# A causal convolution and a low-rank mixer on one core: batch 1 takes the 64-by-32 convolution, with its shifted x copied by DMA

## The chip, the cores and the metric

The kernel runs on one core of a Trainium2 chip. The metric is device time in microseconds (us) of one execution. The kernel before takes 325.4 us (median of three runs, 325.24 to 325.87). The engines of the core are named as in the profile: PE (TensorE, matrix products), PEld (its weight loads), DVE (VectorE), ACT (ScalarE), POOL (GpSimd) and SP (SyncE, which here only issues DMAs).

## The reference

The input x has 8 batches of 4224 rows of 192 channels. Each of 8 heads (24 channels) is convolved along the rows with 7 causal taps, the softmax of the head's weights. The result goes through a low-rank mixing along the rows (U, then V), which is added back, and through a two-layer network per row, which is added too.

```python
def _attn_ref(x, weight):                     # x: 8 x 4224 x 192, weight: 8 heads x 7 taps
    w = weight - np.max(weight, axis=-1, keepdims=True)
    w = np.exp(w)
    w = w / (np.sum(w, axis=-1, keepdims=True) + 1e-09)
    pad = K - 1
    x_pad = np.concatenate([np.zeros((B, pad, D), dtype=np.float32), x], axis=1)
    idx = np.arange(S)[:, None] + np.arange(K)[None, :]
    x_unf = x_pad[:, idx, :].reshape(B, S, K, H, group)
    out = np.einsum('hk,bskhg->bshg', w, x_unf)
    return out.reshape(B, S, D).astype(np.float32)

def _moe_ref(x, U, V, w_ch1, w_ch2):          # U: 4224 x 32, V: 32 x 4224, w_ch1: 192 x 768, w_ch2: 768 x 192
    xt = x.transpose(0, 2, 1)
    h = xt @ U @ V
    u = x + h.transpose(0, 2, 1)
    ch = np.maximum(u @ w_ch1, 0.0) @ w_ch2
    return (u + ch).astype(np.float32)

# reference: _moe_ref(x=_attn_ref(x, weight), U, V, w_ch1, w_ch2)
```

## The kernel before

A batch is 33 tiles of 128 rows, and the 8 batches make 264 tiles, handled in 33 groups of 8. For each batch the steps are: load x (in bfloat16), convolve it into y ("c", or "d" for batch 1), multiply by U ("t"), sum the partial results ("s"). For each group: multiply by V and add to y, giving u, and transpose u by DMA ("h"); then the two layers, `w1` and `w2`. Batches do not end where groups end: group 4 holds the last tile of batch 0 and seven tiles of batch 1, group 8 two tiles of batch 1 and six of batch 2. Batch 0 has a code of its own, ahead of all this, which the change leaves alone.

x of one batch lies in SBUF in blocks of 64 rows: partitions 0 to 63 hold the first 32 blocks, partitions 64 to 127 the other 34. `XP` are the four parts in which a batch is loaded. There are two buffers for x (`xs`, bufs=2), one for the shifted copy of x (`xbs`, bufs=1), three for y, seven for u, five for the transposed u, and eight PSUM banks.

```python
    NB0 = 32
    NB1 = S // HB - NB0

    def x_tile(b):
        xt[b] = xs.tile([P, NB1 + 1, D], BF16, name="x_sb")

    def x_zero(b, eng):
        eng.memzero(xt[b][0:HB, 0, :])

    def x_part(b, r, s0, s1):

        blk = NB0 * r + s0 - 1
        return nc.gpsimd.dma_start(
            out=xt[b][HB * r : HB * r + HB, s0:s1, :],
            in_=x[b, blk * HB : (blk + s1 - s0) * HB, :].rearrange("(j p) d -> p j d", p=HB),
        )

    XP = [(0, 1, 17), (0, 17, NB0 + 1), (1, 0, 18), (1, 18, NB1 + 1)]
```

There are two forms of the convolution. `conv` takes tiles of 64 rows by 64 columns of PE and needs, for every block, the block itself and the one before it, with two matrices of weights. `conv32` takes tiles of 64 by 32 and computes 32 output rows at a time from a window of 64 rows that holds all that they need. For every second group of 32 output rows this window is a block of x as loaded; for the others it is moved by 32 rows, and for these `x_shift` makes a second copy of x on GpSimd, in six steps: partitions 0 to 31 and 64 to 95 from the next block ("same"), partitions 32 to 63 and 96 to 127 from the same block ("ahead", written over what "same" put there). Both forms issue 64 matmuls and 16 evictions for a batch; the string `engs` says which engine (A: ACT, D: DVE) evicts.

```python
    xbt = [None] * B

    def x_shift(b):


        xbt[b] = xbs.tile([P, NB1, D], BF16, name="xb_sb")

        def same(s0, s1, *rest):
            def step():
                nc.gpsimd.tensor_copy(out=xbt[b][:, s0:s1, :], in_=xt[b][:, s0 + 1 : s1 + 1, :])
                for t0, t1 in rest:
                    nc.gpsimd.tensor_copy(
                        out=xbt[b][HB : HB + QB, t0:t1, :],
                        in_=xt[b][HB : HB + QB, t0 + 1 : t1 + 1, :],
                    )

            return step

        def ahead(r, s0, s1):
            def step():
                q = slice(HB * r + QB, HB * r + HB)
                nc.gpsimd.tensor_copy(out=xbt[b][q, s0:s1, :], in_=xt[b][q, s0:s1, :])

            return step

        m = NB0 // 2
        return [
            same(0, m),
            same(m, NB0, (NB0, NB1)),
            ahead(0, 0, m),
            ahead(0, m, NB0),
            ahead(1, 0, m),
            ahead(1, m, NB1),
        ]

    steps = []

    def conv32(b, h0, nh, engs):


        if yt[b] is None:
            yt[b] = ys.tile([P, NT, D], BF16, name="y_sb")
        nk = (NB0 // 2, NB1 // 2)
        for n in range(nh):
            h = h0 + n
            hs = slice(h * GS, h * GS + GS)
            pp = [bank(), bank()]
            for cg in range(4):
                t, w, st = (
                    (xt[b], bands[h // HQ][:, h % HQ, QB : 2 * QB], 1 + cg // 2)
                    if cg % 2
                    else (xbt[b], band2[:, h, :], cg // 2)
                )
                for r in range(2):
                    hr = slice(HB * r, HB * r + HB)
                    nc.tensor.matmul(
                        out=pp[r][QB * cg : QB * cg + QB, 0 : nk[r] * GS],
                        lhsT=w[hr],
                        rhs=t[hr, st : st + 2 * nk[r] - 1 : 2, hs],
                        start=True,
                        stop=True,
                        tile_position=(HB * r, QB * cg),
                    )
            # ... (two evictions, to yt[b] for the two halves, on engs[(2 * n + part) % len(engs)])

    def conv(b, h0, nh, rs, engs, ks=((0, NB0 // 2), (0, NB1 // 2)), pp=None):

        nk = {r: ks[r][1] - ks[r][0] for r in rs}
        if pp is None:
            pp = {r: bank() for r in rs}
        w = nh * GS
        for hh in range(nh):
            h = h0 + hh
            for halo in range(2):
                for r in rs:
                    for c in range(2):
                        st = 1 - halo + c + 2 * ks[r][0]
                        last = nc.tensor.matmul(
                            out=pp[r][HB * c : HB * c + HB, 0 : nk[r] * w].rearrange(
                                "p (k a) -> p k a", a=w
                            )[:, :, hh * GS : hh * GS + GS],
                            lhsT=bands[h // HQ][
                                HB * r : HB * r + HB, h % HQ, HB * halo : HB * halo + HB
                            ],
                            rhs=xt[b][HB * r : HB * r + HB, st : st + 2 * nk[r] - 1 : 2, h * GS : h * GS + GS],
                            start=(halo == 0),
                            stop=(halo == 1),
                            tile_position=(HB * r, HB * c),
                        )
        # ... (one eviction for each r, as in conv32)
        return last
```

The parts of a group, and the two layers:

```python
    # h_group(g): 8 matmuls (tiles of 32 by 128) into 4 or more banks, then DVE's additions to y, which give u

    def transp(g):
        uTt[g] = uts.tile([P, 4, 3, P], BF16, name="uT")
        return nc.sync.dma_start_transpose(
            out=uTt[g][:].rearrange("p i c t -> p (i c) t"),
            in_=ut[g][:].rearrange("p i c f k -> p (i c f k)"),
        )

    # ... (yT_part and hT_part: groups 0 and 1, transposed on PE)

    RELU = ["AD", "AD", "AA", "AD", "AD", "AD"]
    RELU0 = ["AA", "AD", "AA", "AD", "AA", "AD"]

    def w1(g, pat):
        rl = rls.tile([P, MC, 2, 4 * P], BF16, name="rl_sb")
        rlt[g] = rl
        ends = []
        # ... (order: for each m of MC = 6 the three c; pps: its banks)
        for m, c in order:
            if c == 0:
                pps[m] = [bank(), bank()]
            for hf in range(2):
                last = nc.tensor.matmul(
                    out=pps[m][hf][:],
                    lhsT=W1_sb[HB * hf : HB * hf + HB, c, m * P : (m + 1) * P],
                    rhs=uTt[g][HB * hf : HB * hf + HB, :, c, :],
                    start=(c == 0),
                    stop=(c == 2),
                    tile_position=(HB * hf, 0),
                )
            if c < 2:
                continue
            pp = pps[m]
            ends.append(last)
            # ... (relu of the two banks into rl, on ACT or DVE as pat[m] says)
        return ends

    # ...

    def w2(g, t0, n):

        hf, i = t0 // 4, t0 % 4
        cps = bank()
        for a in range(n):
            for m in range(MC):
                last = nc.tensor.matmul(
                    out=cps[:, a * D : (a + 1) * D],
                    lhsT=rlt[g][:, m, hf, (i + a) * P : (i + a + 1) * P],
                    rhs=W2_sb[:, m, :],
                    start=(m == 0),
                    stop=(m == MC - 1),
                )
        done_w2.append(last)
        # ... (DVE adds cps to u and gives o)
        # ... (the 192 KB of o are written out from SyncE's queue)
```

The order of the work is a list of slots. A slot has the groups whose `w1` runs, the groups whose `w2` runs after these, and what is put ahead of the quarter p of the `w2`s (a quarter is `w2` on two tiles, 12 matmuls). `LOADS` says after which matmuls of which `w1` the parts of a batch are loaded.

```python
    def x_load(b, q, after):
        if q == 0:
            x_tile(b)
            x_zero(b, nc.gpsimd)
        held(x_part(b, *XP[q]), after)

    SLOTS = [
        ([0], [], {}),
        ([1], [0], {0: ["h0"], 1: ["h3", "l2:2"], 2: ["l2:3"]}),
        ([2], [1], {0: ["d1", "h1"], 1: ["t1"], 3: ["s1"], 4: ["h4", "x2:6"]}),
        ([3], [2], {1: ["h5"], 3: ["h6"]}),
        (
            [4, 5],
            [3, 4, 5],
            {
                0: ["h7"],
                2: ["c2:0:3:AAD"],
                3: ["c2:3:3:AAD"],
                4: ["c2:6:2:A", "x3:4"],
                6: ["t2"],
                8: ["s2"],
                9: ["h8"],
                11: ["h9"],
            },
        ),
    ]
    nh = 10
    for k in range(5, 14):
        gs = list(range(3 * k - 9, 3 * k - 6))
        hs = [f"h{g}" for g in range(nh, min(nh + 3, NG))] + [None] * 3
        nh = min(nh + 3, NG)
        if k == 5:
            at = {
                2: ["c3:0:3:AAD"],
                3: ["c3:3:3:AAD"],
                4: ["c3:6:2:A", "x4:3"],
                5: [hs[0]],
                6: ["t3"],
                8: ["s3", hs[1]],
                11: [hs[2]],
            }
        elif k < 10:
            b = k - 2
            at = {
                1: [f"c{b}:0:3:AAD"],
                2: [f"c{b}:3:3:AAD"],
                3: [f"c{b}:6:2:A"] + ([f"x{b + 1}:3"] if b + 1 < B else []),
                5: [f"t{b}", hs[0]],
                7: [f"s{b}"],
                8: [hs[1]],
                11: [hs[2]],
            }
        else:
            at = {0: [hs[0]], 4: [hs[1]], 8: [hs[2]]}
        SLOTS.append((gs, gs, {p: [w for w in what if w] for p, what in at.items()}))
    assert nh == NG

    LOADS = {2: [(1, 5), (1, 5)], 3: [(4, 1), (4, 4), (5, 1), (5, 4)]}
    for b in range(4, B):
        g = 3 * b - 6
        LOADS[b] = [(g, 0), (g, 3), (g + 1, 0), (g + 1, 3)]

    # ... (batch 0; the first part of batch 1 is loaded here, the other three at its end)

    def do(what):
        if what[0] == "c":
            b, h0, n, engs = what[1:].split(":")
            conv32(int(b), int(h0), int(n), engs)
            return
        if what[0] == "d":
            for h in range(H):
                last = conv(int(what[1:]), h, 1, [0, 1], "AA" if h == 2 else "AD")
            held(transp(3), last)
            return
        if what[0] == "l":
            b, q = (int(v) for v in what[1:].split(":"))
            x_load(b, q, done_w2[-1])
            return
        if what[0] == "x":
            b, n = (int(v) for v in what[1:].split(":"))
            steps.extend(x_shift(b))
            for _ in range(n):
                steps.pop(0)()
            return
        n = int(what[1:])
        if what[0] == "h":
            h_group(n)
            if n > 1 and n != 3:
                transp(n)
        elif what[0] == "t":
            tt_split(n, tt_mm(n, range(NT)))
        else:
            tt_sum(n)

    for gs1, gs2, at in SLOTS:
        for g in gs1:
            ends = w1(g, RELU0 if g == 1 else RELU)
            for b, blocks in LOADS.items():
                for q, (gb, m) in enumerate(blocks):
                    if gb == g:
                        x_load(b, q, ends[m])
                        if steps:
                            steps.pop(0)()
            if g == 0:
                do("h2")
        while steps and gs1 != [3]:
            steps.pop(0)()
        npc = 4 * len(gs2)
        for p in range(npc + 1):
            for what in at.get(p, []):
                do(what)
            if p < npc:
                g, k = gs2[p // 4], p % 4
                if g == NG - 1 and k == 3:
                    w2(g, 6, 1)
                    w2(g, 7, 1)
                else:
                    w2(g, 2 * k, 2)
```

## Time and profile before

| Quantity | Value |
|---|---|
| Time, median of three | 325.4 us |
| Span of the profiled execution | 323.5 us |
| PE busy | 317.1 us (98%) |
| DVE busy | 269.1 us (83%) |
| ACT busy | 170.4 us (53%) |
| POOL busy | 142.7 us (44%) |
| Granted PE clock | 1.00 over the whole span |
| DMA | 53.52 MB, mean 165 GB/s |

The span is the time between the first and the last instruction in the trace; the time of a run is a little longer than it. "Busy" adds up the time in which an engine has an instruction under way; matmuls overlap, so a busy PE is not PE at its peak. In the lists of groups and in the timeline a row gives the line of the kernel (L554 is `w1`'s matmul, L583 `w2`'s, L369 `conv`'s, L339 `conv32`'s, L457 `h_tiles`', L402 the product with U), the engine, the operation, out<-in with their shapes, and how often it ran. A timeline row starts with the start and the length in us and ends, in brackets, with the idle time of the engine ahead of it and what ended it. L256 and L258 are the evictions to y on ACT and DVE; L568 and L570 those of `w1`; L293, L295 and L305 are the copies of `x_shift`; L79 is the issue of a load of x.

### The profile page before, as it was taken

The numbers are of one execution on the slowest core, as the hardware profiler recorded it, in microseconds if no ns is written. First come the engines' busy times: TensorE is split into PE (matmuls) and PEld (weight loads), VectorE is DVE, ScalarE is ACT, GpSimd is POOL, SyncE is SP. The second block draws the span as 40 slices with busy tenths as digits, with TensorE's granted clock in tenths as the row PEclk, the third lists the DMA queues.
The fourth block names the chain that finished last, engine by engine and source line by source line (L and its number), as shares of the span: only waits on it lengthen the run. The fifth ranks groups of instructions, "written<-read, shape, count | busy, mean of one in ns | idle before, by whom it ended". The sixth has DMA issues, their size and how long they took to land.

```text
span 323.5 us, 9584 instructions
## 1 busy us (share of the span) xinstructions
PE 317.1 (98%) x3996; PEld 223.2 (69%) x3996; DVE 269.1 (83%) x551; ACT 170.4 (53%) x344; POOL 142.7 (44%) x111
## 2 busy tenths in 40 slices
PE   6999999999999999999999999999999999999996
PEld 3757676478677647866864784587797497487495
DVE  6769989987977986998798699879898897896864
ACT  1766624860874397088339708824903902912920
POOL 8664179729947694786859497000000000000000
PEclk9999999999999999999999999999999999999999
DMA  8999993999996899699699976139269059048035
GB/s 104 192 192 178 209 211 99 203 195 248 210 153 180 229 175 169 170 162 195 166 238 183 192 162 181 33 112 244 58 168 267 8 149 268 25 121 271 2 119 176
DMA packets 122907, 53.52 MB, mean 165 GB/s; under 512 B 87760, under 2 KB 122832, under 8 KB 122864
## 3 DMA queue, kind: packets, MB, share of 16 engines
q1 hardware_dynamic: 84528, 38.08, 47.0%
q0 software_dynamic: 38192, 14.73, 39.6%
q8 instruction: 31, 0.51, 0.7%
q14 instruction: 12, 0.10, 0.1%
q10 hardware_dynamic: 144, 0.10, 0.1%
HBM read 29.49 MB, written 25.95 MB: 171 GB/s over the span
## 4 chain that ended last, share of the span: by engine, by line
PE 92%; ACT 3%; DMA 2%; DVE 1%; issue 0%; POOL 0%; POOLq 0%
PE ps L583 42%; PE ps L554 39%; PE ps L339 3%; PE ps L457 3%; DMA x_sb<-in_x_dram 2%; PE ps L402 2%; ACT rl_sb L568 2%; PE ps L369 1%; ACT y_sb L256 1%; PE ps L509 1%; DVE u_sb L479 1%; DVE rl_sb L570 1%; PE ps L524 0%; PE ps L428 0%; POOL x_sb L79 0%
## 5 line engine op out<-in xcount | busy, mean ns | idle before, releaser
L568 ACT ACTIVATE rl_sb<-ps 128x512 bf16<-128x512 f32 x233 | 124.3, 603 | 108.0 <-PE ps L554 96.0
L583 PE MATMUL ps<-W_sb,rl_sb 128*128 128x192 bf16 x1584 | 141.9, 246 | 0.2
L583 PEld LDWEIGHTS <-rl_sb 128*128 128x128 bf16 x1584 | 128.1, 98 | 13.5 <-issue 13.1
L554 PE MATMUL ps<-uT,W_sb 64*128 64x512 bf16 x1188 | 131.7, 376 | 0.0
L570 DVE TENSOR_SCALAR rl_sb<-ps 128x512 bf16<-128x512 f32 x163 | 105.3, 688 | 15.7 <-PE ps L554 15.4
L554 PEld LDWEIGHTS <-W_sb 64*128 64x128 bf16 x1188 | 66.9, 94 | 60.5 <-issue 3.9
L592 DVE TENSOR_TENSOR out_sb<-ps,u_sb 128x384 f32<-128x384 f32 (+1 forms) x133 | 70.4, 550 | 25.9 <-PE ps L583 25.4
L305 POOL COPY xb_sb<-x_sb 32x3072 bf16<-32x3072 bf16 (+1 forms) x24 | 67.6, 2826 | 0.7
L479 DVE TENSOR_TENSOR u_sb<-y_sb,ps 128x192 bf16<-128x192 bf16 (+1 forms) x168 | 66.3, 461 | 0.0
L293 POOL COPY xb_sb<-x_sb 128x3072 bf16<-128x3072 bf16 x12 | 32.6, 2744 | 34.6 <-PE ps L339 25.7
L256 ACT ACTIVATE y_sb<-ps 128x384 bf16<-128x384 f32 (+4 forms) x90 | 38.2, 514 | 10.7 <-PE ps L339 7.9
L79 POOL DMA_DIRECT2D x_sb<-in_x_dram x32 | 27.1, 849 | 17.5 <-PE ps L554 10.5
L258 DVE CAST y_sb<-ps 128x408 bf16<-128x408 f32 (+4 forms) x36 | 19.2, 578 | 1.1 <-PE ps L369 0.9
L457 PE MATMUL ps<-tt_sb,V_sb 32*128 32x192 bf16 x264 | 12.4, 246 | 0.1
L339 PE MATMUL ps<-xb_sb,band 64*32 64x384 bf16 x192 | 12.1, 332 | 0.0
L339 PE MATMUL ps<-x_sb,band 64*32 64x384 bf16 x192 | 12.1, 333 | 0.0
L457 PEld LDWEIGHTS <-V_sb 32*128 32x128 bf16 x264 | 4.7, 92 | 7.3 <-issue 7.3
L416 ACT ACTIVATE tt_hi<-ps 128x192 bf16<-128x192 f32 x8 | 2.6, 331 | 10.9 <-PE ps L402 10.9
L369 PE MATMUL ps<-x_sb,band 64*64 64x240 bf16 (+3 forms) x192 | 8.1, 276 | 0.3 <-DMA x_sb<-in_x_dram 0.3
L369 PEld LDWEIGHTS <-band 64*64 64x64 bf16 x192 | 6.0, 106 | 2.2 <-issue 1.5
L339 PEld LDWEIGHTS <-band 64*32 64x32 bf16 x384 | 4.5, 89 | 4.1 <-issue 3.0
L402 PE MATMUL ps<-y_sb,U_sb 128*32 128x192 bf16 x258 | 7.4, 247 | 0.0
(65 smaller groups left out, 69.0 us busy)
## 6 DMA issues: line engine op xcount, KB each, us to landing
out_dram<-out_sb SPq DMA_DIRECT2D x131, 192.0 KB, 2.7
x_sb<-in_x_dram POOLq DMA_DIRECT2D x14, 384.0 KB, 7.3
x_sb<-in_x_dram POOLq DMA_DIRECT2D x7, 432.0 KB, 7.3
x_sb<-in_x_dram POOLq DMA_DIRECT2D x7, 408.0 KB, 8.0
x_sb<-in_x_dram POOLq DMA_DIRECT2D x1, 504.0 KB, 7.6
uT<-u_sb SPq DMA_TRANSPOSE x31, 3.9
x_sb<-in_x_dram POOLq DMA_DIRECT2D x1, 480.0 KB, 5.9
W_sb<-in_moe_w_ch_dram POOLq DMA_DIRECT2D x2, 192.0 KB, 7.6
```

Source lines behind the costliest of these rows:

```text
L79: return nc.gpsimd.dma_start(out=xt[b][HB * r : HB * r + HB, s0:s1, :], in_=x[b, blk * HB : (blk + s1 - s0) * HB, :].rearrange("(j p) d -> ...
L256: nc.scalar.activation(out=out, in_=in_, func=ACT.Copy)
L293: nc.gpsimd.tensor_copy(out=xbt[b][:, s0:s1, :], in_=xt[b][:, s0 + 1 : s1 + 1, :])
L305: nc.gpsimd.tensor_copy(out=xbt[b][q, s0:s1, :], in_=xt[b][q, s0:s1, :])
L339: nc.tensor.matmul(out=pp[r][QB * cg : QB * cg + QB, 0 : nk[r] * GS], lhsT=w[hr], rhs=t[hr, st : st + 2 * nk[r] - 1 : 2, hs], start=True, ...
L457: nc.tensor.matmul(out=banks[pr][:, a * D : (a + 1) * D], lhsT=V_sb[32 * q : 32 * q + 32, (j // 8) * 2 + j % 2, :], rhs=ttb[b][32 * q : 32 ...
L479: nc.vector.tensor_tensor(out=u_group(g)[:, i : i + n, :, hf, :], in0=yt[b][:, run[0] : run[0] + n, :].rearrange("p n (c k) -> p n c k", c=3),
L554: last = nc.tensor.matmul(out=pps[m][hf][:], lhsT=W1_sb[HB * hf : HB * hf + HB, c, m * P : (m + 1) * P], rhs=uTt[g][HB * hf : HB * hf + HB ...
L568: nc.scalar.activation(out=rl[:, m, hf, :], in_=pp[hf][:], func=ACT.Relu)
L570: nc.vector.tensor_scalar_max(out=rl[:, m, hf, :], in0=pp[hf][:], scalar1=0.0)
L583: last = nc.tensor.matmul(out=cps[:, a * D : (a + 1) * D], lhsT=rlt[g][:, m, hf, (i + a) * P : (i + a + 1) * P], rhs=W2_sb[:, m, :], start ...
L592: nc.vector.tensor_tensor(out=o[:, 0:n, :].rearrange("p n (c k) -> p n c k", c=3), in0=cps[:, 0 : n * D].rearrange("p (n c k) -> p n c k", ...
```

## The change

Batch 1 is convolved by `conv32` in place of `conv`. For this its shifted copy of x must be there early, and it is made by DMA inside SBUF and not by GpSimd: eight transfers of 32 partitions each, four on SyncE's queue ("w0", ahead of `w2` of group 0) and four on ACT's ("w1"). The convolution is done in three pieces between the quarters of `w2` of group 1, and not in one. Since `conv32` of batch 1 holds the one buffer for shifted copies, the copy of batch 2 starts after it, and the loads of batch 2 and 3 move: batch 2 from `w1` of group 2 on, batch 3 at the end of slot 3. The transpose of group 3, which was held back until batch 1's convolution, is issued with h3. `w2` of group 3 moves from slot 4 to slot 3, and the h groups, t and s move accordingly; from slot 6 on the list of slots is the same as before.

```diff
--- before.py
+++ after.py
@@ -315,6 +315,16 @@
             ahead(1, 0, m),
             ahead(1, m, NB1),
         ]
+
+    def x_shift_dma(b, n, eng):
+
+        if xbt[b] is None:
+            xbt[b] = xbs.tile([P, NB1, D], BF16, name="xb_sb")
+        for r in range(2):
+            s0, s1 = ((0, NB0 // 2), (NB0 // 2, (NB0, NB1)[r]))[n]
+            for o in (1, 0):
+                q = slice(HB * r + QB * (1 - o), HB * r + QB * (2 - o))
+                eng.dma_start(out=xbt[b][q, s0:s1, :], in_=xt[b][q, s0 + o : s1 + o, :])
 
     steps = []
 
@@ -617,39 +627,49 @@
 
 
     SLOTS = [
-        ([0], [], {}),
-        ([1], [0], {0: ["h0"], 1: ["h3", "l2:2"], 2: ["l2:3"]}),
-        ([2], [1], {0: ["d1", "h1"], 1: ["t1"], 3: ["s1"], 4: ["h4", "x2:6"]}),
-        ([3], [2], {1: ["h5"], 3: ["h6"]}),
+        ([0], [], {0: ["w0"]}),
+        ([1], [0], {0: ["w1", "h0"], 1: ["h3"]}),
+        (
+            [2],
+            [1],
+            {
+                0: ["h1"],
+                2: ["c1:0:3:AAD"],
+                3: ["c1:3:3:AAD"],
+                4: ["c1:6:2:AD", "x2:5"],
+            },
+        ),
+        ([3], [2, 3], {0: ["t1"], 1: ["s1"], 2: ["h4"], 5: ["h5"], 7: ["l3:0", "l3:2", "p", "l3:1", "l3:3"]}),
         (
             [4, 5],
-            [3, 4, 5],
+            [4, 5],
             {
-                0: ["h7"],
-                2: ["c2:0:3:AAD"],
-                3: ["c2:3:3:AAD"],
-                4: ["c2:6:2:A", "x3:4"],
+                0: ["h6"],
+                2: ["c2:0:2:A"],
+                3: ["c2:2:3:AAD"],
+                4: ["c2:5:3:AAD", "x3:4"],
+                5: ["h7"],
                 6: ["t2"],
-                8: ["s2"],
-                9: ["h8"],
-                11: ["h9"],
+                7: ["s2"],
+                8: ["h8"],
             },
         ),
     ]
-    nh = 10
+    nh = 9
     for k in range(5, 14):
         gs = list(range(3 * k - 9, 3 * k - 6))
-        hs = [f"h{g}" for g in range(nh, min(nh + 3, NG))] + [None] * 3
-        nh = min(nh + 3, NG)
+        hs = [f"h{g}" for g in range(nh, min(nh + 4, NG))] + [None] * 3
+        nh = min(nh + (4 if k == 5 else 3), NG)
         if k == 5:
             at = {
-                2: ["c3:0:3:AAD"],
-                3: ["c3:3:3:AAD"],
-                4: ["c3:6:2:A", "x4:3"],
-                5: [hs[0]],
+                0: [hs[0]],
+                2: ["c3:0:2:A"],
+                3: ["c3:2:3:AAD"],
+                4: ["c3:5:3:AAD", "x4:3"],
+                5: [hs[1]],
                 6: ["t3"],
-                8: ["s3", hs[1]],
-                11: [hs[2]],
+                8: ["s3", hs[2]],
+                11: [hs[3]],
             }
         elif k < 10:
             b = k - 2
@@ -667,7 +687,7 @@
         SLOTS.append((gs, gs, {p: [w for w in what if w] for p, what in at.items()}))
     assert nh == NG
 
-    LOADS = {2: [(1, 5), (1, 5)], 3: [(4, 1), (4, 4), (5, 1), (5, 4)]}
+    LOADS = {2: [(2, 0), (2, 1), (2, 3), (2, 5)]}
     for b in range(4, B):
         g = 3 * b - 6
         LOADS[b] = [(g, 0), (g, 3), (g + 1, 0), (g + 1, 3)]
@@ -766,10 +787,9 @@
             b, h0, n, engs = what[1:].split(":")
             conv32(int(b), int(h0), int(n), engs)
             return
-        if what[0] == "d":
-            for h in range(H):
-                last = conv(int(what[1:]), h, 1, [0, 1], "AA" if h == 2 else "AD")
-            held(transp(3), last)
+        if what[0] == "w":
+            n = int(what[1:])
+            x_shift_dma(1, n, (nc.sync, nc.scalar)[n])
             return
         if what[0] == "l":
             b, q = (int(v) for v in what[1:].split(":"))
@@ -781,10 +801,13 @@
             for _ in range(n):
                 steps.pop(0)()
             return
+        if what == "p":
+            steps.pop(0)()
+            return
         n = int(what[1:])
         if what[0] == "h":
             h_group(n)
-            if n > 1 and n != 3:
+            if n > 1:
                 transp(n)
         elif what[0] == "t":
             tt_split(n, tt_mm(n, range(NT)))
@@ -795,7 +818,7 @@
         for g in gs1:
             ends = w1(g, RELU0 if g == 1 else RELU)
             for b, blocks in LOADS.items():
-                for q, (gb, m) in enumerate(blocks):
+                for q, (gb, m) in zip((0, 2, 1, 3) if b == 2 else range(4), blocks):
                     if gb == g:
                         x_load(b, q, ends[m])
                         if steps:
```

## The prediction

> **What bounds the kernel now.** I began with the busy shares and the chain of work that ended last, to see which engine sets the time.
>
> ```profile
> PE 317.1 (98%) x3996; PEld 223.2 (69%) x3996; DVE 269.1 (83%) x551; ACT 170.4 (53%) x344; POOL 142.7 (44%) x111
> ...
> PE 92%; ACT 3%; DMA 2%; DVE 1%; issue 0%; POOL 0%; POOLq 0%
> ```
>
> PE is in the chain for 92% of the span; a change pays only where it shortens PE's own sequence or takes a wait out of it. So I looked in the chain, in order of time (start, length, what), for where PE is not the link:
>
> ```profile
> 33.92 2.09 PE ps L554 x18
> 36.02 2.54 ACT rl_sb L568 x5
> 38.56 3.10 ACT y_sb L256 x8
> 41.70 1.15 PE ps L583 x12
> ...
> 95.16 0.64 PE ps L339 x19
> ```
>
> For 5.6 us, around the convolution of batch 1, the chain runs over ACT's evictions; the conv of a later batch (L339, at 95.16) is 0.64 us of plain PE. The timeline of that stretch says what happens:
>
> ```profile
> 37.84 3.24 PE L369 MATMUL ps<-x_sb,band 64*64 64x384 bf16 x64
> 38.44 3.59 ACT L256 ACTIVATE y_sb<-ps 128x384 bf16<-128x384 f32 x9
> 38.59 3.51 DVE L258 CAST y_sb<-ps 128x408 bf16<-128x408 f32 x7
> ...
> 41.02 0.63 PE L457 MATMUL ps<-tt_sb,V_sb 32*128 32x192 bf16 x8
> ...
> 48.84 2.29 PEld L554 LDWEIGHTS <-W_sb 64*128 64x128 bf16 x23 [0.44 <-DVE u_sb L479]
> ```
>
> All 16 results of batch 1's conv leave PSUM in one burst: ACT and DVE are busy for the whole of it, and PE goes at their pace. The h matmuls behind it (41.02) take 0.68 us to the next w2 at 41.70, where others take 0.27 to 0.35. The last line is a smaller loss: the W1 of group 3 comes directly after h4 and waits for DVE's additions.
>
> GpSimd's timeline shows what else the change touches, the shifted copy of x:
>
> ```profile
> 42.52 5.43 POOL L293 COPY xb_sb<-x_sb 128x3072 bf16<-128x3072 bf16 x2 [8.89 <-DMA x_sb<-in_x_dram]
> 48.01 0.50 POOL L295 COPY xb_sb<-x_sb 32x384 bf16<-32x384 bf16 x1
> 48.56 11.25 POOL L305 COPY xb_sb<-x_sb 32x3072 bf16<-32x3072 bf16 x4
> ...
> 71.39 5.43 POOL L293 COPY xb_sb<-x_sb 128x3072 bf16<-128x3072 bf16 x2 [6.20 <-PE ps L339]
> ...
> 87.52 3.08 POOL L305 COPY xb_sb<-x_sb 32x3456 bf16<-32x3456 bf16 x1
> ```
>
> One shifted copy costs GpSimd 5.43 + 0.50 + 11.25 = 17.2 us. There is no room for that between the landing of batch 1 (about 31 us) and its conv; that is why batch 1 takes the other conv, and why the change makes this copy by DMA.
>
> **What the Trainium skill says.** "TensorEngine Tiling (Array Packing)", section Tiling Modes, gives 4 independent tiles for 64x64 and 8 for 64x32. The trace agrees: 64 matmuls of the same widths take 3.18 us in batch 1 and 0.64 + 0.71 + 0.47 = 1.82 us in batch 3, though part of the 3.18 is the wait for evictions. Its section PSUM Bottleneck warns that packing speeds up the matmuls and not the evacuation; that fits ACT and DVE here, and the change spreads the evictions over three places. "SBUF — State Buffer", section Door 1: The DMA port swizzle, says that 32 partitions reach 8 of 16 ports and gives 189 GB/s for 1 MiB. No run here shows a copy inside SBUF yet. "DMA: Bandwidth & Descriptors", section Issuing engines are not separate DMA queues, says that two issuing queues share the same 16 engines, so I take the two queues to save issue time, not transfer time. The trace of before has GpSimd's and SyncE's queues overlapping, at 194 to 225 GB/s in all, which doesn't contradict it.
>
> **Part by part, on PE.** (1) The conv of batch 1: 3.18 us (37.84 to 41.02) goes, 1.82 us (measured on batch 3) comes: gain 1.36. (2) h1 now follows W1 of group 2, not the burst: 0.68 to about 0.34, gain 0.34. (3) W1 of group 3 now comes after a conv piece and not after h4: 4.33 us (47.22 to 51.55) to about 3.99, as group 2's W1 took: gain 0.34. (4) W1 of groups 4 and 5 took 8.17 us where three groups take 11.76 later (3.92 each), so up to 0.33 is there; I count 0.1. (5) Batch 2's conv took 0.94 + 0.64 + 0.47 = 2.05 us; with its first piece cut to two heads for ACT alone I count 0.2. (6) h8 now stands right ahead of W1 of group 6, as h4 stood ahead of group 3's: loss 0.35. Sum: 1.36 + 0.34 + 0.34 + 0.1 + 0.2 - 0.35 = 2.0 us. t1, s1, the h groups and all w2 are moved, not removed; from the slot after c3 on, the program is the same as before.
>
> **Part by part, beside PE.** I laid the new order out with the measured lengths (a w2 of 12 matmuls 0.99 to 1.10 us, h 0.3, t 0.85, s 0.16) from 33.85, where W1 of group 2 starts in both: W1 to 37.84, h1 and two w2 to 40.2. So conv 1 begins at 40.2 and ends at 44.2; W1 of group 3 to 48.2; w2 of groups 2 and 3 with t1, s1, h4, h5 to 58.2; W1 of groups 4 and 5 to 66.2; conv 2 from 68.6 to 72.5; W1 of group 6 at 78.6 (before: 81.17); conv 3 at 92.9 (before: 95.08). Four transfers have to meet these times.
>
> (a) The DMA copy of batch 1. Its x lands at about 21.0, 26.2, 28.5 and 31.2 (issues at 12.29, 19.20, 21.24 and 22.1, plus 8.7, 7.0, 7.3 and 9.1 to landing). It moves 128 partitions x 33 blocks on average x 384 B = 1.6 MB. SyncE's half starts at about 29, behind group 2's transpose (issued 27.24 to 28.99), ACT's at about 31. With the page's 189 GB/s the 1.6 MB take an estimated 8.6 us: done at about 38 to 39 beside output writes and the loads of batch 2, against 40.2. Slack 1 to 2 us. ACT issues its four in a gap: it waited 4.43 us there until 34.71.
>
> (b) Transpose of group 4. h4 ends at about 51.7, its additions 2 us later, and transposes land 3.9 us (median) after issue: 57.6, against W1 of group 4 at 58.2. Slack 0.6 us.
>
> (c) The copy of batch 2 on GpSimd. Loads issue at about 34.3 to 38.7 in place of 29.4 to 33.6; landing as before some 11 to 12 us after the last issue gives 50. Then 2.72 + 0.50 + 3 x 2.74 + two loads of batch 3 (1.84) + 3.08 = 16.4 us: 66.4, against conv 2 at 68.6. Slack 2.2 us.
>
> (d) The copy of batch 3. The last two loads now issue after (c), to about 68.1, and land 8.8 us later at 76.9. Then 2.72 + 0.50 + 2 x 2.74 + 2.74 + 3.08 and two issues with a memset (1.8) = 16.3 us: 93.2, against conv 3 at 92.9. Slack about zero: before it was 95.08 - 90.60 = 4.5 us, and the new order takes four w2 from between the two convs.
>
> I charge 0.15 us for (a), 0.15 for (b), 0.05 for (c) and 0.15 for (d), my weighting of small stalls with even or lower odds. Gain 2.0 - 0.5 = 1.5 us; 325.4 - 1.5 = **323.9 us**.
>
> **Rivals.** First: the DMA copy takes the place of the evictions as the bound. For it: at half the estimated rate 1.6 MB take 17 us and end at about 47, and PE stands 6 to 7 us at conv 1: 330 us. Against it: batch 2's loads now stay out of the way until 34.3, and rows of 6 KB are long against the 384 B of the loads. Second: GpSimd's chain becomes the bound: loads of batch 2 slower by 3 us push (c) over its slack and (d) 2 to 3 us past conv 3: 325.5 to 327. For it: one load of batch 2 already took 12.2 us to land; against it: after 39 only output writes compete. Third: everything is hidden and even (d) meets its time, and the later W1 blocks lose nothing: 323.2. Fourth: DVE (83% busy) holds the new slots, since six of the 16 evictions and all additions still fall to it; in the slot of conv 1 I count 5 x 0.69 (W1) + 1.94 (h1) + 4 x 0.55 (w2) + 6 x 0.53 (conv) = 10.8 us of DVE against 10.4 of PE. A backlog of half a microsecond would eat a third of the gain: 324.5.
>
> **Range and chances.** The third rival sets the low end, 322.9 with some play; the second and fourth together the high end, 325.2; the first lies outside, at 5 to 8%. Two per cent are 6.5 us: no gain of that size is in the chain, and only a stall of the whole first rival reaches it. Faster by over 2%: 0.01; within: 0.97; slower: 0.02.
>
> **What would show it.** Right: no L369 matmul of width 384 or 408, 64 more of L339 near 40 to 44 us in three pieces of 0.45 to 0.75 us; ACT no longer a link of the chain at 36 to 41; W1 of group 3 near 44.2 and W1 of group 6 near 78.6. Wrong: PE waiting at an L339 for a DMA into xb_sb (rival 1) or for a POOL copy (rival 2), at an L554 for the transpose of group 4, or rows of L554 waiting for DVE u_sb or y_sb.

## The result and the profile after

The changed kernel takes **337.7 us** (median of six runs, 335.2 to 341.2), the kernel before 325.25 us in the same session. The ratio is **1.036** (95% interval 1.032 to 1.040): 12.4 us slower, where 1.5 us of gain was predicted. The profiled execution is the longest of the six, 341.2 us, so its stalls add up to more than the median loss. The page of the changed kernel, busy shares, granted clock and the chain that ended last:

```profile
PE 320.7 (95%) x3996; PEld 220.2 (65%) x3996; DVE 269.4 (79%) x550; ACT 171.0 (50%) x345; POOL 142.8 (42%) x111
...
PEclk9999987999999999999799999999999999999999
...
PE 56%; POOL 20%; DMA 17%; issue 5%; DVE 0%; POOLq 0%
```

Before, PE was in the chain for 92% and every digit of the clock was a 9. Now 37% of the chain are GpSimd and DMA, and the clock dips twice. Three lines of the list of waits (total us, times, longest):

```profile
POOL xb_sb L293 <- DMA x_sb<-in_x_dram: 36.6, 7, 10.3
...
PE ps L564 <- DMA uT<-u_sb: 7.9, 3, 5.7
...
PE ps L349 <- POOL xb_sb L305: 2.8, 2, 2.6
```

The second line is new: in the trace of before PE never waits for a DMA transpose. The timeline of PE shows where (start, length, what, and in brackets the idle time ahead):

```profile
40.57 0.77 PE L349 MATMUL ps<-xb_sb,band 64*32 64x384 bf16 x2
...
44.75 0.33 PE L349 MATMUL ps<-x_sb,band 64*32 64x408 bf16 x1
50.83 6.42 PE L564 MATMUL ps<-uT,W_sb 64*128 64x512 bf16 x36 [5.75 <-DMA uT<-u_sb]
```

The conv of batch 1 went as predicted, in three pieces from 40.6 to 45.1, without a wait that matters for its copies. Then PE stands for 5.75 us in front of W1 of group 3, until the transpose of group 3 lands. After that W1 takes 6.42 us in place of 4.40: the clock is at half for 6.8 us from 48.8 on, 3.7 us after PE fell idle (45.1). That agrees with the Trainium skill, "TensorE: Matmul & The Clock Gate", Part 1, which has the clock fall to half after about 3.4 us of idling. The other dip followed a shorter idle time: a wait of 2.59 us, which ended at 163.8, was enough.

Where the rest went is read from the starts of W1, beside those of an experiment told below, the changed kernel with the loads of x cut to almost nothing from batch 2 on:

| W1 of group | before, us | changed | changed, loads cut | the loads' share (changed less loads cut) | what was added since the row above |
|---|---|---|---|---|---|
| 2 | 33.9 | 33.8 | 33.9 | 0 | |
| 3 | 47.2 | 50.8 | 44.7 | 6.1 | wait for the transpose of group 3, 5.75 |
| 4 | 56.4 | 67.8 | 59.4 | 8.4 | W1 of group 3 at half clock, 2.3 |
| 6 | 81.2 | 88.6 | 79.9 | 8.7 | |
| 9 | 109.5 | 119.3 | 108.7 | 10.6 | wait for the transpose of group 7, 1.96 |
| 12 | 137.5 | 147.9 | 136.7 | 11.2 | |
| 15 | 165.8 | 180.6 | 165.0 | 15.6 | conv of batch 5: 8.5 us for 4.1 (wait for GpSimd's copy 2.59, then half clock) |
| 30 | 296.5 | 311.3 | 295.7 | 15.6 | |
| span | 323.5 | 339.4 | 323.8 | 15.6 | |

So nearly all of it is three stalls and two stretches at half clock. The first stall is in the timeline above; the other two are (PE's timeline):

```profile
94.60 7.94 PE L564 MATMUL ps<-uT,W_sb 64*128 64x512 bf16 x72 [1.96 <-DMA uT<-u_sb]
...
163.82 0.33 PE L349 MATMUL ps<-xb_sb,band 64*32 64x408 bf16 x1 [2.59 <-POOL xb_sb L305]
```

Each stall waits, directly or through GpSimd, for a transfer. The issue times tell why the first came. SyncE's timeline, changed kernel and then before:

```profile
28.91 4.85 SPq L327 DMA_DIRECT2D xb_sb<-x_sb  x4
33.88 1.56 SPq L610 DMA_DIRECT2D out_dram<-out_sb  x1
35.53 3.78 SPq L508 DMA_TRANSPOSE uT<-u_sb  x1
```

```profile
41.13 1.53 SPq L498 DMA_TRANSPOSE uT<-u_sb  x1
```

The transpose of group 3 is issued 5.6 us sooner than before and lands 4.4 us later: 50.8 against 46.4. It stands in SyncE's queue behind four copies and an output. The DMA issues of 35 to 40 us in the changed kernel, and those of 28 to 47 us in the kernel before (KB each, median us from issue to landing):

```profile
x_sb<-in_x_dram POOLq DMA_DIRECT2D x1, 408.0 KB, 20.8
...
uT<-u_sb SPq DMA_TRANSPOSE x1, 15.3
```

```profile
x_sb<-in_x_dram POOLq DMA_DIRECT2D x1, 408.0 KB, 12.2
uT<-u_sb SPq DMA_TRANSPOSE x2, 5.3
```

The last load of batch 2 takes 20.8 us in place of 12.2, the transpose 15.3 in place of 5.2. Over the whole run, before has 8 transposes with a load of x in flight for more than half of their time (median 7.7 us, up to 9.2) and 23 others (median 3.3, up to 5.0). So the collision was there before; what is new is that PE waits for it.

The queues of the changed kernel from 31 to 39 us, and from 40 to 60 us (packets, MB, time of the packets as a share of 16 engines' window):

```profile
q1 hardware_dynamic: 1236, 1.05, 58.1%
q10 hardware_dynamic: 173, 0.82, 51.1%
```

```profile
q0 software_dynamic: 4352, 1.65, 73.5%
q1 hardware_dynamic: 3593, 1.85, 52.5%
```

Up to 39 us, while the copies run, the loads' queue (q0) doesn't appear at all, though three loads of batch 2 are issued from 35.0 to 36.9. All 1.65 MB of batch 2 move after 40 us, in 4352 packets, at once with the transpose and the outputs in q1, whose own landings take 10.7 us (median) in that window. "DMA: Bandwidth & Descriptors", section Queues, rings and completion order, says that an engine goes round its queues packet by packet. From 40 us on the trace fits that: from 48 to 52 us each of the two queues moves 1012 packets. From 35 to 39 us it doesn't show the newly issued loads getting a turn, and why not stays open; what the turns do to loads that are already under way, the third experiment shows.

### The profile page after: what moved, and what is told of

Its sections match the earlier page's. It is cut to its first block, busy times and chain, and to the rows that moved or that the text cites. A ratio compares the mean times of both kernels' runs of the same rounds, so it can differ in the third digit from the quotient of the medians.

```text
span 339.4 us, 9610 instructions
## 1 busy us (share of the span) xinstructions
PE 320.7 (95%) x3996; PEld 220.2 (65%) x3996; DVE 269.4 (79%) x550; ACT 171.0 (50%) x345; POOL 142.8 (42%) x111
## 4 chain that ended last, share of the span: by engine, by line
PE 56%; POOL 20%; DMA 17%; issue 5%; DVE 0%; POOLq 0%
PE ps L593 29%; PE ps L564 22%; DMA x_sb<-in_x_dram 15%; POOL xb_sb L305 12%; POOL x_sb L79 4%; POOL xb_sb L293 2%; PE ps L349 2%; DMA Ur<-in_moe_U_dram 2%; PE ps L467 2%; PE ps L412 1%; POOL band L780 1%; POOL xb_sb L295 0%; POOL x_sb L74 0%; PE ps L438 0%; POOL W_sb L137 0%
## 5 line engine op out<-in xcount | busy, mean ns | idle before, releaser
L564 PE MATMUL ps<-uT,W_sb 64*128 64x512 bf16 x1188 | 133.7, 381 | 8.6 <-DMA uT<-u_sb 7.9
L593 PEld LDWEIGHTS <-rl_sb 128*128 128x128 bf16 x1584 | 128.7, 98 | 14.1 <-issue 13.3
L564 PEld LDWEIGHTS <-W_sb 64*128 64x128 bf16 x1188 | 64.3, 95 | 74.0 <-DMA uT<-u_sb 9.9
L256 ACT ACTIVATE y_sb<-ps 128x408 bf16<-128x408 f32 (+4 forms) x91 | 38.6, 510 | 18.1 <-PE ps L349 15.3
L349 PE MATMUL ps<-xb_sb,band 64*32 64x384 bf16 (+1 forms) x224 | 15.5, 342 | 2.9 <-POOL xb_sb L305 2.8
L349 PE MATMUL ps<-x_sb,band 64*32 64x384 bf16 x224 | 14.5, 343 | 0.0
L467 PE MATMUL ps<-tt_sb,V_sb 32*128 32x192 bf16 x264 | 12.4, 246 | 0.0
L349 PEld LDWEIGHTS <-band 64*32 64x32 bf16 x448 | 5.6, 91 | 8.5 <-issue 7.0
L153 PE MATMUL ps<-zz 128*128 128x512 f32 (+1 forms) x10 | 6.0, 743 | 1.1 <-DVE zz L143 1.1
L412 PEld LDWEIGHTS <-U_sb 128*32 128x32 bf16 x258 | 5.4, 96 | 1.7 <-issue 1.4
## 6 DMA issues: line engine op xcount, KB each, us to landing
x_sb<-in_x_dram POOLq DMA_DIRECT2D x7, 408.0 KB, 10.3
```

The source lines that it names most:

```text
L256: nc.scalar.activation(out=out, in_=in_, func=ACT.Copy)
L349: nc.tensor.matmul(out=pp[r][QB * cg : QB * cg + QB, 0 : nk[r] * GS], lhsT=w[hr], rhs=t[hr, st : st + 2 * nk[r] - 1 : 2, hs], start=True, ...
L467: nc.tensor.matmul(out=banks[pr][:, a * D : (a + 1) * D], lhsT=V_sb[32 * q : 32 * q + 32, (j // 8) * 2 + j % 2, :], rhs=ttb[b][32 * q : 32 ...
L564: last = nc.tensor.matmul(out=pps[m][hf][:], lhsT=W1_sb[HB * hf : HB * hf + HB, c, m * P : (m + 1) * P], rhs=uTt[g][HB * hf : HB * hf + HB ...
L593: last = nc.tensor.matmul(out=cps[:, a * D : (a + 1) * D], lhsT=rlt[g][:, m, hf, (i + a) * P : (i + a + 1) * P], rhs=W2_sb[:, m, :], start ...
```

## The experiments

I began with two theories: that the eight copies did the damage (A), or the new order and the new places of the loads, which would do it without any copy (B). Later expectations say which reading they test. Times of the kernel before on the same chips were 325.3 us; a ratio is to that kernel, with its 95% interval.

### The changed kernel without the copies

```diff
-                    else (xbt[b], band2[:, h, :], cg // 2)
+                    else (xbt[b] if b != 1 else xt[b], band2[:, h, :], cg // 2)
@@ what[0] == "w"
-            x_shift_dma(1, n, (nc.sync, nc.scalar)[n])
+            pass
```

The copies are left out; the conv of batch 1 reads x as loaded where it should read the shifted copy. Its work on PE is the same.

> The changed kernel with the eight copies of batch 1 left out; its convolution reads x as loaded for both windows, so that batch 1 of the output is left wrong, with the same number and shape of matmuls. Theory A (the copies block the DMA queues from 29 to 39 us, and outputs, the transpose of group 3 and batch 2's loads pile up behind them): W1 of group 3 starts near 45 us, no half-clock stretch, 323 to 325.5 us. Theory B (the loads of batch 2, moved to 34 us, collide with the transpose of group 3 by themselves): W1 of group 3 still waits some us, 330 us or more.

Measured: **335.6 us** (334.2 to 337.6), ratio 1.030 (1.026 to 1.035). W1 of group 3 starts at 44.1 without a wait, so the first stall does come from the copies. Yet little is won, since the loss moves. The loads of batch 3, issued from 65.2 to 70.7, now land as late as 85.0, and the transposes of groups 6 and 7 beside them take 10.5 and 10.3 us. PE's timeline:

```profile
88.17 1.03 PE L564 MATMUL ps<-uT,W_sb 64*128 64x512 bf16 x4 [3.78 <-DMA uT<-u_sb]
```

W1 of group 7 then takes 7.0 us at half clock, and the conv of batch 4 waits 2.59 us for GpSimd's copy and runs to 8.3 us. "The copies are the whole cause" falls: they decide which transpose is hit, not whether one is. B falls in its early wait too.

### The changed kernel with batch 2's loads where they were

```diff
-        ([1], [0], {0: ["w1", "h0"], 1: ["h3"]}),
+        ([1], [0], {0: ["w1", "h0"], 1: ["h3", "l2:2"], 2: ["l2:3"]}),
-    LOADS = {2: [(2, 0), (2, 1), (2, 3), (2, 5)]}
+    LOADS = {2: [(1, 5), (1, 5)]}
```

> The changed kernel with the copies, but batch 2's loads where the kernel before has them (issues from 29.4 us on). Theory A: the copies now share the queues with these loads and end later, PE waits at batch 1's convolution or at W1 of group 3, 328 us or more. Theory B: the collision of late loads and transpose is gone, 323.5 to 326 us.

Measured: **335.6 us** (332.1 to 339.4), ratio 1.026 (1.019 to 1.034). Loads and copies now go at once: the last copy lands at 43.5 and not at 40.8, the conv of batch 1 waits 3.04 us for it, and the transpose of group 3 takes 15.9 us. Earlier loads don't help; the copies and the loads together are too much before 47.

### The kernel before with the copies added

```diff
-        ([0], [], {}),
-        ([1], [0], {0: ["h0"], 1: ["h3", "l2:2"], 2: ["l2:3"]}),
+        ([0], [], {0: ["w0"]}),
+        ([1], [0], {0: ["w1", "h0"], 1: ["h3", "l2:2"], 2: ["l2:3"]}),
```

With `x_shift_dma` and its "w" as in the change. Nothing reads the copies: conv, order and loads stay as before.

> The kernel before with the eight copies added as dead work on the same two queues at the same places; no convolution reads them. Theory A: outputs and the transpose of group 3 are delayed, 327 us or more. Theory B: the copies are hidden, 325 to 326 us.

Measured: **335.5 us** (334.6 to 336.0), ratio 1.029 (1.027 to 1.032). The copies end at 44.1. The transpose of group 3, still issued behind the conv, lands at 55.2, 11.1 us after its issue:

```profile
55.24 1.04 PE L564 MATMUL ps<-uT,W_sb 64*128 64x512 bf16 x4 [7.99 <-DMA uT<-u_sb]
```

7.99 us of wait, and W1 of group 3 at half clock for a part (5.5 us). W1 of group 6 is 9.1 us late, and it stays at that. So 1.6 MB of extra transfer, beside loads at their old places, cost 10 us. How the copies hold up the loads is seen in the queues from 38 to 41 us (packets, MB); q0 is the loads', q1 and q10 carry the copies:

```profile
q10 hardware_dynamic: 78, 0.36, 53.7%
q1 hardware_dynamic: 77, 0.33, 46.2%
q0 software_dynamic: 81, 0.03, 8.5%
```

The three queues move nearly the same number of packets. But two thirds of the copies' packets are rows of 6 to 7 KB, and those of the loads are of 384 B, so the loads get a third of the turns and 4% of the bytes; from 34 to 37 us, nearly alone, they had moved 1122 packets. They land as late as 54.9, and the transpose is in flight beside them.

### The kernel before with only the loads moved

```diff
-        ([1], [0], {0: ["h0"], 1: ["h3", "l2:2"], 2: ["l2:3"]}),
+        ([1], [0], {0: ["h0"], 1: ["h3"]}),
-    LOADS = {2: [(1, 5), (1, 5)], 3: [(4, 1), (4, 4), (5, 1), (5, 4)]}
+    LOADS = {2: [(2, 0), (2, 1), (2, 3), (2, 5)], 3: [(4, 1), (4, 4), (5, 1), (5, 4)]}
```

The four parts are issued in the order of the change; there is no copy by DMA.

> The kernel before, its conv of batch 1 and its slots unchanged and no copies, but batch 2's loads at the places of the change (from 34 us on). Theory C: the transpose of group 3, issued at 41 us into the loads, takes 8 us or more, and W1 of group 3 waits at 47.2; 327 to 334 us. Theory D: no copies, no delay, 325 to 326 us.

Measured: **331.8 us** (331.4 to 333.2), ratio 1.021 (1.018 to 1.024). Same issue of the transpose (41.2), no copy anywhere, and it takes 9.9 us beside the loads:

```profile
51.13 1.46 PE L554 MATMUL ps<-uT,W_sb 64*128 64x512 bf16 x6 [3.78 <-DMA uT<-u_sb]
```

Either part alone costs: the copies 10 us, the later loads 6.5, the change with its order but no copies 10. Together they cost 12.4, so the parts don't add up; each is enough to use up the slack of that transpose, which in the trace of before is 47.2 - 46.4 = 0.8 us.

### The change's order with the old conv in pieces

```diff
+            if b == "1":
+                for i in range(int(n)):
+                    conv(1, int(h0) + i, 1, [0, 1], "AD" if i != 1 else "AA")
+                return
             conv32(int(b), int(h0), int(n), engs)
@@ what[0] == "w"
-            x_shift_dma(1, n, (nc.sync, nc.scalar)[n])
+            pass
```

With the loads of batch 2 where they were before, and the six steps of its copy in one go; a `conv` for each head, at the places of the three pieces.

> The changed kernel's slots without any copy: batch 1's convolution with 64-by-64 tiles, in three pieces with the evictions spread as in the change, batch 2's loads as before. If the spread of the evictions and the new order bring most of what was expected of the change, and the narrower tiles only 0.8 us, 324 to 325 us; if the new order itself leaves too little time for GpSimd's copies (rival 2 of the prediction), 326 us or more.

Measured: **327.1 us** (325.5 to 331.1, 20 runs), ratio 1.006 (1.003 to 1.008). Without copies and late loads nearly all of the loss is gone, and nothing is gained. The transpose of group 3, issued at 34.0 in the midst of the loads, takes 11.9 us and lands at 45.9; W1 of group 3 starts at 46.0. The lead of 1.3 us is nearly gone by W1 of group 6 (81.0, before 81.2), and at W1 of group 15 the profiled execution is 1.8 us behind; PE waits up to 0.61 us for transposes and, at 152.4, 0.91 us for GpSimd's copy. That is the prediction's second rival, in a mild form.

### The changed kernel with the loads cut

```diff
     def x_tile(b):
+        if b in (2, 3):
+            xt[b] = xt[b - 2]
+            return
@@ x_load
-        held(x_part(b, *XP[q]), after)
+        r, s0, s1 = XP[q]
+        held(x_part(b, r, s0, s0 + 1 if b in (2, 3) else s1), after)
```

Every part of batches 2 and 3 loads one block and no more, into the buffer of the batch two before; the rest of their x is left out. Copies, issues and waits stay.

> The changed kernel with its copies, but of the loads of batches 2 and 3 only one block per part (1/16 to 1/18 of the bytes; the rest of these batches' x is left as batches 0 and 1 had it, so that two batches of the output are left wrong). Theory C (a transpose by DMA and a load of x that are in flight together slow each other, transposes from 3 to 5 us to 8 to 16): the transpose of group 3, only held up behind the copies, lands by 43 us, W1 of group 3 starts at 45 without a wait, transposes of groups 6 and 7 take under 5 us, 323 to 326 us. Theory D (the copies by themselves hold the transpose back): W1 of group 3 still waits 4 us or more, 329 us or more.

Measured: **326.6 us** (325.6 to 330.4, 20 runs), ratio 1.004 (1.001 to 1.006). The transpose of group 3 still takes 8.8 us behind the copies, but lands at 44.4, in time for W1 at 44.9; those of groups 6 to 8 take 3.2. The same cut for all of batches 2 to 7 (`b > 1` in place of `b in (2, 3)`) was made in both kernels, the changed one and the one before:

> The changed kernel with its copies, but from batch 2 on every part of x is loaded as one block only (the rest of the buffers keeps batches 0 and 1; six batches of the output are left wrong). Theory C (loads and transposes in flight together slow each other): no transpose over 7 us but that of group 3 behind the copies, no wait over 1 us, 323 to 325 us. If the prediction's sum for PE was right, 2.0 us under the next kernel; if the order itself loses part of it (0.9 us were waited at W1 of group 4 with batches 2 and 3 cut), 0.3 to 1.

> The kernel before, with the loads cut in the same way. Its transposes then take 3 to 5 us, but their slack had hidden the 7 to 9 us already: 324.5 to 325.3 us, the same as before. If loads cost time in another way than through transposes, 2 us or more under the kernel before.

Measured: the changed kernel **325.56 us** (ratio 1.0002, 0.9989 to 1.0015), the kernel before **325.36 us** (1.0001, 0.9986 to 1.0016). The changed kernel loses its whole 12 us; the kernel before loses nothing, so in it the loads were hidden. The landing times of all transposes of each, changed and then before:

```profile
DMA to landing us min/median/max: 3.2/3.9/7.2
```

```profile
DMA to landing us min/median/max: 3.2/3.8/5.2
```

With the loads in, these lines read 3.2/4.2/15.3 and 3.2/3.9/9.2. The 7.2 is the transpose of group 3, behind the copies; W1 of group 3 no longer waits for it (PE's timeline of the changed kernel with all loads cut):

```profile
44.73 4.06 PE L567 MATMUL ps<-uT,W_sb 64*128 64x512 bf16 x36
```

This shows that the loss needs the bytes of the loads; the landing times show how, through transfers in flight together. How much of the loss comes by the transposes and how much by GpSimd's copies, which wait for the loads too, it doesn't separate. It also bounds the change: even with next to no loads it is no faster than the kernel before.

### The clock, warmed

```diff
         for g in gs1:
+            if g == 3:
+                wps = bank()
+                idle(6)
             ends = w1(g, RELU0 if g == 1 else RELU)
```

`idle` issues matmuls on zeros, which nobody reads, ahead of W1 of group 3.

> The changed kernel with 12 dummy matmuls on zeros (about 5 us of PE work) in program order just ahead of W1 of group 3, where PE waits 5.75 us. If the wait costs a second time because PE's clock falls to half, W1 of group 3 takes 4.1 us and not 6.4, and the time is 2 to 3 us under the change's. If the 6.4 us come from the evictions, the time is the same or up to 1 us longer.

Measured: **341.0 us** (338.7 to 341.6), ratio 1.047 (1.043 to 1.051). PE's timeline:

```profile
45.54 4.46 PE L153 MATMUL ps<-zz 128*128 128x512 f32 x10
50.69 4.06 PE L564 MATMUL ps<-uT,W_sb 64*128 64x512 bf16 x36 [0.70 <-DMA uT<-u_sb]
```

The same transpose lands as late, but W1 takes 4.06 us and not 6.42, and W1 of group 4 starts at 65.5 and not 67.8: the 2.3 us are the clock's. They aren't kept: the time is 3.3 us above the change's, not 2 to 3 under it. At the convs of batches 3 and 4 PE now waits 1.38 and 2.71 us for GpSimd's copies, and the clock is at half for 6.8 us from 133.6 on. In this trace what comes later is set by GpSimd, which waits for the loads as before (the last of batch 2 lands at 58.9), and not by PE's early loss.

### GpSimd's copies left out

```diff
     def x_shift(b):
+        if b > 2:
+            return [lambda: None] * 6
@@ conv32
-                    else (xbt[b], band2[:, h, :], cg // 2)
+                    else (xbt[b] if b < 3 else xt[b], band2[:, h, :], cg // 2)
```

From batch 3 on the shifted copy is left out; the convs read x as loaded.

> The changed kernel, but from batch 3 on GpSimd makes no shifted copy; the convolution reads x as loaded (five batches of the output are left wrong), loads as in the change. Theory E (after the first delay GpSimd's loop of load and copy has no slack, holds the delay and adds to it where PE then waits and its clock halves): no wait at a convolution, W1 of group 15 some 28 us after that of group 12, 330 to 333 us. If the later loss comes from transposes and loads alone, 335 us or more.

Measured: **340.1 us** (339.1 to 346.6), ratio 1.044 (1.042 to 1.046); the profiled execution took 346.6 us, so only its order of events is used. No conv waits any more, and W1 of groups 12 and 15 start 28.3 us apart, as before the change (32.7 in the changed kernel). The expected total was missed by far: the free GpSimd issues the loads of batch 4 from 90.4 on, not 96.7, into the transpose of group 8, which takes 14.1 us; PE waits 8.56 us. Taking one wait away moved the loads onto another transpose.

### The halves of the partitions, and a spread conv

```diff
-        for r in range(2):
+        for r in (0, 1) if n == 0 else (1, 0):
```

ACT's four copies begin with the upper 64 partitions, so that the two queues work on different halves.

> The changed kernel, only ACT's four copies begin with the upper 64 partitions, so that the two queues work on different halves of SBUF. If the copies are limited by the ports of 32 partitions (203 GB/s seen from 33 to 40 us), they end 2 us or more earlier than 40.8, the transpose of group 3 lands earlier by as much and the time falls by 2 to 5 us. If they are limited by the 16 engines or by issue, they end at 40 to 41 and the time is that of the change, 335 to 339 us.

Measured: **335.3 us** (334.6 to 337.0), ratio 1.032 (1.029 to 1.035). The copies got no faster: SyncE's copies land by 38.4, ACT's by 47.5. ACT's issues were themselves held (31.2, 31.9, 33.7, 38.2), and its evictions behind them: PE waits 1.97 us within W1 of group 2. Whether the 32 partitions limit the copies stays open.

```diff
# the kernel before; "d" takes heads and engines, the transpose of group 3 stays behind the last
-        ([1], [0], {0: ["h0"], 1: ["h3", "l2:2"], 2: ["l2:3"]}),
-        ([2], [1], {0: ["d1", "h1"], 1: ["t1"], 3: ["s1"], 4: ["h4", "x2:6"]}),
+        ([1], [0], {0: ["h0"], 1: ["h3", "l2:2"], 2: ["l2:3", "d1:0:2:A"], 3: ["d1:2:2:A"], 4: ["d1:4:2:A"]}),
+        ([2], [1], {0: ["d1:6:2:AD", "h1"], 1: ["t1"], 3: ["s1"], 4: ["h4", "x2:6"]}),
```

The aim of the change, the burst of evictions, without a copy or a moved load.

> The kernel before with batch 1's conv (64-by-64 tiles) cut in four pieces of two heads, three of them between the w2 of group 0, evicted by ACT alone, which is idle there; loads, slots and the hold on the transpose of group 3 (until the last piece) as before. No copies. If the burst of evictions was worth what the prediction counted (0.5 us of conv, 0.34 of h1), 324.3 to 325 us; if the transpose of group 3 then lands with batch 2's loads at 45 to 46 us and holds W1 of group 3 there, the gain stays under 1 us; a loss if it lands later than 46.4.

Measured: **326.1 us** (326.0 to 326.5), ratio 1.002 (1.001 to 1.004). The pieces take 1.31 + 3 x 0.88 us on PE, no better than 3.24 in one burst; W1 of group 3 starts at 48.0 (before: 47.2). No version of these beats the kernel before.

## Why the prediction was wrong

**What bounds the kernel** was read rightly: PE's own sequence, with about 2 us of burst in it. It was the measure of the gain, not of the risk.

**On PE.** W1 of group 3 was laid out at 44.2; without the first stall it starts at 44.1 (no copies) or 44.7 (loads cut). W1 of group 6 was laid out at 78.6 and starts at 79.9 with the loads cut. By W1 of group 9 that kernel is 0.8 us ahead of before, not 2.0: 0.5 had gone by group 3, and 0.71 was a wait for the transpose of group 4, which took 4.8 us where I had taken the median, 3.9, against a slack of 0.6. Its last matmul ends at 319.48 (before: 320.28), but the span ends 4.3 us after that and not 3.2. So of 2.0 us nothing would have reached the end: with the loads cut the two kernels take 325.56 and 325.36 us.

**(a) The copies** were nearly right: the last landed at 40.8, estimated 38 to 39, and conv 1, begun at 40.6, barely felt it. From the first landing (33.8) to the last (40.8) the other seven copies, 1.43 MB, took 7.0 us: 204 GB/s, near the estimate's 189. But ACT's four issues didn't fit the gap that ends at 34.71: they went on until 35.35.

**(b) to (d) are where it failed.** Each transfer's time to landing was taken from the kernel before, as if it belonged to the transfer: "landing as before some 11 to 12 us after the last issue", "transposes land 3.9 us (median)". Measured: 20.8 us for the last load, and 15.3, 4.8, 9.9 and 6.7 us for the transposes of groups 3, 4, 6 and 7. Those numbers belonged to a schedule that mostly kept loads and transposes apart, and the change brings them together. My sentence "after 39 only output writes compete" had it the wrong way round: after 39 the loads, the transpose and the outputs are all in flight.

**The transpose of group 3 was left out** of the four transfers. The old code held it back until behind the conv, and I took its release as harmless; in fact the change puts it behind four copies and, issued at 35.5, among the loads of batch 2, issued from 35.0 to 38.8. It was the first stall.

**The rivals.** The first had little more than a third of the size (330) and the wrong wait: PE stood at W1 for a transpose, not at the conv for a copy. The fourth, DVE, shows in no wait for u or y. The second, GpSimd's chain, is the later part of the loss. Its timeline in the changed kernel:

```profile
50.02 2.74 POOL L293 COPY xb_sb<-x_sb 128x3072 bf16<-128x3072 bf16 x1 [10.30 <-DMA x_sb<-in_x_dram]
59.69 2.74 POOL L293 COPY xb_sb<-x_sb 128x3072 bf16<-128x3072 bf16 x1 [6.93 <-DMA x_sb<-in_x_dram]
```

Two waits for loads of batch 2, 17.2 us in all: the copy of batch 2 ends at 76.2 and not at the 66.4 of (c). For batch 5, whose last three loads took 11.4 to 13.7 us, it ends at 163.8, when conv 5 had begun at 160.9. After that no conv waits any more, and the loss stays as it is (from W1 of group 15 to that of group 30 both kernels take 130.7 us): PE, 98% busy before, has no idle time in which to catch up. The half clock behind the longer stalls, which I had not counted, adds 1.4 to 2.9 us a time (W1 5.5 to 7.0 us for 4.1).

**Open.** The end comes 1.1 us later after the last matmul because the last output writes land later: the last two, of 96 KB each, take 2.9 and 2.8 us in the changed kernel with all loads cut, and 1.7 each before. Why they are slower was not tried. The late end is in every trace of a kernel here that convolves batch 1 with the 64-by-32 form, but also in that of the kernel before with its loads cut (4.2 us), so that form is not shown to be the reason. And the times of the changed kernel run from 335 to 341 us; only the longest execution has a trace, so which stall is smaller in the others isn't shown.

## What to carry to other kernels

The time of a transfer from issue to landing belongs to what is in flight beside it: before loads are moved, list for each moment which transposes, copies and loads will overlap, and give each wait a slack for the slowest landing seen, not for the median. A hold on a transfer that looks needless may be what keeps two kinds of transfer apart. A gain of 1 or 2 us on the bounding engine isn't worth the slack of a transpose that every later stage waits for; cutting the transfers to almost nothing, in both kernels, shows at once how much of a loss is theirs.

## What had not been expected of the hardware

- A DMA transpose of one group took 3.2 to 5.0 us with little or no loading beside it (the kernel before) and up to 15.9 us beside loads and copies (the second experiment); a load of 408 KB took 12.2 us in the kernel before, 20.8 in the changed one and 25.7 in the second experiment.
- While copies of long rows ran, loads of 384 B rows that were issued from 35.0 on moved no packet before 40 (the changed kernel). Loads already under way got as many packets through as each of the copies' queues, and 4% of the bytes (the third experiment).
- The issue itself grew: SyncE was 3.78 us at one transpose (1.53 before), ACT 5.76 us at three copies. With the halves exchanged that held up ACT's evictions, and PE waited 1.97 us for them.
- Short waits of PE came before the half clock: 2.59 us (the changed kernel), 1.97 and 1.91 us (the copies with halves exchanged). It did not follow the wait of 1.96 us at W1 of group 7, nor those of 2.08 and 2.07 us in the second experiment, so the length of the wait alone doesn't decide.
